# A scheduler's rule for where float32 subtractions run: beside GpSimd's instructions, and on GpSimd

## The chip, the core and the metric

The kernel runs on one core of a Trainium2 chip. The metric is the device time of one execution in microseconds. The core's engines are TensorE (PE; its weight loads are shown as PEld), VectorE (DVE), ScalarE (ACT), GpSimd (POOL) and SyncE (SP, which here issues nearly all DMAs).

## What is computed

Decay attention over 4 batches, 8 heads, 576 positions and a head width of 64, and then two feed-forward layers, all in float32. Cut to what matters:

```python
scores = scale * q @ k.T                       # per batch and head
scores = where(causal, -1e9, scores + cum[:, None] - cum[None, :])
attn = softmax(scores);  x = attn @ v          # 2304 tokens x 512
h1 = x @ w1_in;   y1 = (h1 * sigmoid(1.702 * h1)) @ w1_out       # 512 -> 2048 -> 512
h2 = y1 @ w2_in;  out = (max(h2, 0) + alpha * min(h2, 0)) @ w2_out
```

## The kernel before, in words

A matmul operand is split into two float32r tiles: a rounded copy (the high part) and the difference of the source and that copy (the low part). A product is three matmuls: high by high, high by low, low by high. So each operand costs a copy and a **float32 subtraction** of equal size, and where the Strassen form of a product is used (the last third of the first layer, and the second layer) there are more additions and subtractions to make its operands.

The program is written as a list of operations with read and write sets. `Plan.plan` orders it: at each step it takes, of the operations whose inputs are ready, the one that can start first. An operation has one or more alternatives, tuples of engine, estimated duration, a bias that is added to the end time when engines are compared, and a flag `port`. Operations with the flag share one resource, `free["port"]`: no two of them are planned at the same time, on whatever engine. VectorE's reads of PSUM are planned without it. The engines then execute their queues in the order that the plan gave; the times of the plan are not kept, only its order.

The places that the prediction speaks of:

- `a_sub` (the subtraction's alternatives): GpSimd with the flag; VectorE with a bias of `BS` = 200 ns and the flag. Once the attention phase and the last third of the first product are written down, the list `late` is filled, and from there on `a_sub` gives VectorE alone, with the flag.
- `exact` (lines 685 to 688) rebuilds a weight tile `wc` from its raw bits `wraw`: two ScalarE passes, a shift on VectorE (line 687) and an integer add on VectorE or GpSimd (line 688). `halves` then makes the weight's high and low part (`w`; the copy by line 513 or 515, the subtraction by line 518). 16 weight tiles are made so during the first 110 us, while attention runs.
- `split` makes `KA` and `QA`, the operands of the scores, out of the transposed `tk`; `gemm1` makes `xh` and `xl` out of the attention output `xr`, and multiplies them with `w` (line 1008). These matmuls are planned as background work that fills TensorE's gaps in the attention phase.
- `tail` is the Strassen form for the last 768 tokens of the first product. It starts when attention has ended: `st` (line 1115) are combinations of `xr`, `xt` the split operands; for each pair of weight tiles `tw` and `td` (line 1140) are sums of weights, `tb` the split form of `td`. Its products are line 1031, its PSUM sums line 1057. The rest of the background matmuls of line 1008 is interleaved with it.
- The matmuls of attention are lines 872 and 878 (scores), 952 (transposes) and 966 (times v); line 891 adds the mask on VectorE, line 900 is the exponential on ScalarE, and line 919 (VectorE or GpSimd) or 917 (ScalarE) scales the result.
- Where the plan of the first 130 us leaves TensorE idle, `run` puts filler matmuls in (line 484).

Of the kernel before, what the change touches and what calls it, by code (L numbers as in the profile page):

```python
# [12 lines left out]
ALU = mybir.AluOpType  # L13
# [3 lines left out]
BC = 0  # L17
WC = 0.6
WO_ = 0.0
BS = 200  # L20
WS = 0
BD = 300
WLAG = 2500.0
# [226 lines left out]
def kernel(  # L250
# [51 lines left out]
    plan = Plan()  # L302
    E = {"PE": nc.tensor, "DVE": nc.vector, "ACT": nc.scalar, "POOL": nc.gpsimd, "SP": nc.sync, "ACTQ": nc.scalar}
# [195 lines left out]
    def c_dve(n, fast=False):  # L499
        return n / (1.92 if fast else 0.96) + 68.0  # L500
# [4 lines left out]
    def c_act(n, ps=False):  # L505
        return n / 1.2 + (51.0 if ps else 93.0)

    def c_pool(n):
        return 2.1 * n + 200.0
# [19 lines left out]
    late = []  # L529

    def a_sub(n):
        if late:
            return [("DVE", c_dve(n), 0.0, True)]
        return [("POOL", c_pool(n), 0.0, True), ("DVE", c_dve(n), BS + WS * n, True)]

    plan.add(DMA(BH * S * 4), lambda e: nc.sync.dma_start(f_sb(), f.rearrange("b h s -> (b h) s")), (), [b_f], -100)

# [84 lines left out]
    for part, (lo, hi) in enumerate(((0, SPLIT), (SPLIT, S))):  # L622
        ts_ = [t for t in range(NKT) if lo <= t * P < hi]
        pri = -80 if part == 0 else A0 + P1PRI
# [45 lines left out]
    def hold(o, gate):  # L670

        if gate is not None and gate not in o.deps:
            o.deps.add(gate)
            gate.succ.append(o)

    def exact(src, pri, lpri=None, lag=0.0, gate=None):

        raw, w = Buf(p_raw8), Buf(p_wc)
        n = KT * P
        o = plan.add(DMA(P * n * 8), lambda e: nc.sync.dma_start(raw.ap.rearrange("p c n t -> p c (n t)"), src), (), [raw], pri if lpri is None else lpri, lag)  # L680
        hold(o, gate)
        low, high = lambda: raw.ap[:, :, :, 0], lambda: raw.ap[:, :, :, 1]
        wi = lambda: w.ap.bitcast(I32)

        plan.add([("ACT", c_act(n))], lambda e: nc.scalar.activation(w.ap, high().bitcast(F32), AF.Prelu, scale=2.0 ** -112, alpha=2.0 ** 32), [raw], [w], pri)
        plan.add([("ACT", c_act(n))], lambda e: nc.scalar.mul(low(), low().bitcast(U32), 2.0 ** -29), (), [(raw, 0)], pri)
        plan.add([("DVE", c_dve(n, True), 0.0, True)], lambda e: nc.vector.tensor_scalar(wi(), wi(), 3, None, op0=ALU.logical_shift_left), (), [w], pri)  # L687
        plan.add(a_sub(n), lambda e: E[e].tensor_tensor(wi(), wi(), low(), op=ALU.add), [raw], [w], pri)  # L688
        return w

    def halves(n, src, sb_, hi, lo, buf, key, pri, over=()):

        plan.add(a_copy(n), lambda e: copy(e, hi(), src()), sb_, [(buf, (key, 0)), *over], pri)
        plan.add(a_sub(n), lambda e: sub(e, lo(), src(), hi().bitcast(F32)), [*sb_, (buf, (key, 0))], [(buf, (key, 1)), *over], pri)

    def in_rows(w, m):
        return w[:, m * P:(m + 1) * P].bitcast(I32).rearrange("(c p) n -> p c n", p=P)

    def out_rows(w, m):
        return w[m * P:(m + 1) * P, :].bitcast(I32).rearrange("p (c n) -> p c n", c=KT)  # L700
# [21 lines left out]
    def split(T, w, big, keys, pri):  # L722
        hi, lo = Buf(None, big, 0), Buf(None, big, 1)
        plan.add(a_copy(w), lambda e: copy(e, hi.ap[:, :w], T.ap[:, :w]), [T], [(hi, x) for x in keys], pri)
        plan.add(a_sub(w), lambda e: sub(e, lo.ap[:, :w], T.ap[:, :w], hi.ap[:, :w].bitcast(F32)), [T, *((hi, x) for x in keys)], [(lo, x) for x in keys], pri)
        return hi, lo
# [461 lines left out]
    def first_weights():  # L1188
        over = {3: p_k0.bufs[:2], 4: p_k0.bufs[2:], 5: p_d0.bufs, 6: p_q0.bufs[:2], 7: p_q0.bufs[2:], 8: p_v0.bufs, 9: p_v0.bufs, **{m: p_r0.bufs[:4] if m < 13 else p_r0.bufs[4:] for m in range(10, NM)}}
        for m in range(NM):  # L1190
            WI[m] = Buf(wA)
            pri = A0 + WPRI + m * WSTEP
            w = exact(in_rows(w1_in, m), pri, A0 + WPRI - 1 + m * WSTEP, WLAG + (1000.0 if m < 4 else 0.0))
            halves(KT * P, lambda w=w: flat(w.ap), [w], lambda m=m: flat(WI[m].ap[:, 0]), lambda m=m: flat(WI[m].ap[:, 1]), WI[m], 0, pri, over.get(m, ()))
# [38 lines left out]
    for k in range(NM):  # L1233
        WO[k] = wb = Buf(wo[k >= WO0])
        pri = 1500.0 + k
        w = exact(out_rows(w1_out, k), pri)
        halves(KT * P, lambda w=w: flat(w.ap), [w], lambda wb=wb: wb.ap[:, 0], lambda wb=wb: wb.ap[:, 1], wb, 0, pri, [WI[k]])
# [64 lines left out]
    for p in range(NPAIR):  # L1302
        TS[p] = sw = Buf(wS)
        pri = 5000.0 + p
        w = [exact(in_rows(w2_in, m), pri, None, WLAG, Y[34 + 4 * p] if p < 6 else None) for m in (p, p + NPAIR)]
# [96 lines left out]
    for i, (t0, n) in enumerate(out_turn):  # L1402
# [4 lines left out]
        for k in range(NPAIR):  # L1407
            pri = base + k - 60
            raw, s_, hi, lo = Buf(p_R), Buf(p_S), Buf(p_hi[turn % 2]), Buf(p_lo[turn % 2])
# [96 lines left out]
```

## Time and profile before

| | before |
|---|---|
| median of 3 runs | 953.25 us (951.26 to 953.94) |
| the profiled execution, its own time | 951.31 us |
| its span | 949.6 us |
| TensorE clock granted | 0.998 of full speed |
| busy: PE, DVE, ACT, POOL | 939.9, 739.8, 561.2, 31.2 us |
| POOL instructions with a record | 46 |
| HBM read and written | 107.71 and 63.85 MB |

Matmuls are pipelined and the ends of their records are modelled, so a busy share of 99% of TensorE says that no long gap is shown, not that the engine is at its peak. How dense it is worked is seen from the number of matmuls in a stretch. On VectorE and ScalarE records of neighbours overlap by some 0.08 us, so what one instruction costs in a row of them is the distance between starts. An instruction that is held back by another engine's use of memory shows as a longer record, not as idle time.

### The profile page before, as it was taken

How to read it: one execution, taken by the hardware profiler on the slowest of the kernel's cores; microseconds unless marked ns; L12 is line 12 of the kernel's file. 1: busy time of each engine (PE TensorE's matmuls, PEld its weight loads, DVE VectorE, ACT ScalarE, POOL GpSimd, SP SyncE). 2: the span in 40 equal slices, each digit the busy share in tenths (PEclk: the TensorE clock that was granted, in tenths of full speed). 3: DMA queues.
4: the chain of work that ended last, by engine and by line, in shares of the span. 5: the costliest groups of instructions: out<-in, count | busy, mean ns of one | idle time of the engine just before them, and what ended most of it. 6: DMA issues, size and time to landing. Idle time of an engine off the chain costs nothing.

```text
span 949.6 us, 18126 instructions
## 1 busy us (share of the span) xinstructions
PE 939.9 (99%) x6517; PEld 873.0 (92%) x6517; DVE 739.8 (78%) x1771; ACT 561.2 (59%) x1238; POOL 31.2 (3%) x46
## 2 busy tenths in 40 slices
PE   8999999999999999999999999999999999999998
PEld 6789898889899999988888988999999999999998
DVE  5999997877759658755768876979569878898987
ACT  6999976777664538556776774556466623221212
POOL 1000010201001000000000000000000000000000
PEclk9999999999999999999999999999999999999999
DMA  7777764343211546558896784787638594443423
GB/s 151 172 185 190 180 158 97 85 92 73 59 52 65 183 159 226 157 174 327 299 323 198 257 257 151 257 307 288 244 124 319 187 398 164 139 150 96 155 79 100
DMA packets 179035, 172.78 MB, mean 182 GB/s; under 512 B 98320, under 2 KB 153760, under 8 KB 176640
## 3 DMA queue, kind: packets, MB, share of 16 engines
q1 hardware_dynamic: 178928, 171.61, 57.9%
q8 instruction: 51, 0.84, 0.4%
q14 instruction: 40, 0.33, 0.1%
q10 hardware_dynamic: 16, 0.01, 0.0%
HBM read 107.71 MB, written 63.85 MB: 181 GB/s over the span
## 4 chain that ended last, share of the span: by engine, by line
PE 89%; DVE 5%; DMA 1%; issue 0%; ACT 0%; DVEq 0%; SPq 0%; ACTq 0%
PE bk L1031 25%; PE bk L1252 21%; PE bk L1434 19%; PE bk L1008 12%; PE bk L966 4%; PE bk L952 4%; PE bk L878 3%; PE bk L872 1%; DVE w L518 1%; DVE wc L688 1%; DMA raw<-in_k_dram 1%; DVE eT L515 0%; DVE wc L687 0%; DVE tk L719 0%; DVE eb L891 0%
## 5 line engine op out<-in xcount | busy, mean ns | idle before, releaser
L1031 PE MATMUL bk<-x,wS 128*128 128x384 f32 x912 | 160.4, 334 | 0.0
L1031 PEld LDWEIGHTS bk<-x,wS 128*128 128x128 f32 x912 | 158.2, 188 | 0.7 <-DVE lx L1057 0.5
L1008 PE MATMUL bk<-xh,w 128*128 128x320 f32 (+2 forms) x640 | 150.2, 310 | 0.1
L1252 PE MATMUL bk<-lh,w 128*128 128x512 f32 (+1 forms) x640 | 146.9, 368 | 0.0
L1252 PEld LDWEIGHTS bk<-lh,w 128*128 128x128 f32 x640 | 112.7, 189 | 19.8
L1008 PEld LDWEIGHTS bk<-xh,w 128*128 128x128 f32 x640 | 108.9, 189 | 4.5 <-issue 1.7
L1008 PE MATMUL bk<-xl,w 128*128 128x320 f32 (+2 forms) x320 | 97.0, 303 | 0.4 <-DVE xl L518 0.4
L518 DVE TENSOR_TENSOR ll<-lx,lh 128x512 fp32r<-128x512 f32 (+1 forms) x80 | 50.9, 636 | 40.0 <-PE bk L1252 26.1
L1252 PE MATMUL bk<-ll,w 128*128 128x512 f32 (+1 forms) x320 | 81.2, 368 | 0.0
L513 ACT CAST x<-x 128x768 fp32r<-128x768 f32 (+3 forms) x41 | 33.4, 825 | 67.5 <-PE bk L1434 54.9
L1434 PE MATMUL bk<-wS,x 128*128 128x256 f32 x567 | 70.5, 283 | 0.0
L1218 ACT ACTIVATE lx<-lx 128x512 f32<-128x512 f32 (+1 forms) x80 | 46.9, 588 | 39.5 <-DVE ll L518 34.6
L1434 PEld LDWEIGHTS bk<-wS,x 128*128 128x128 f32 x567 | 69.1, 192 | 0.0
L1434 PE MATMUL bk<-wS,lh 128*128 128x256 f32 x378 | 68.7, 283 | 0.0
L1252 PEld LDWEIGHTS bk<-ll,w 128*128 128x128 f32 x320 | 57.0, 189 | 9.6
L1008 PEld LDWEIGHTS bk<-xl,w 128*128 128x128 f32 x320 | 60.5, 189 | 0.7 <-DVE xl L518 0.7
L513 ACT CAST lh<-x 128x768 fp32r<-128x768 f32 (+3 forms) x29 | 23.2, 805 | 62.9 <-PE bk L1434 48.3
L518 DVE TENSOR_TENSOR x<-x,x 128x768 fp32r<-128x768 f32 (+3 forms) x59 | 55.9, 979 | 4.1 <-ACT x L513 3.1
L1434 PEld LDWEIGHTS bk<-wS,lh 128*128 128x128 f32 x378 | 59.0, 192 | 0.0
L513 ACT COPY lx<-bk 128x384 f32<-128x384 f32 x72 | 34.3, 481 | 38.6 <-PE bk L1031 25.6
L1434 PE MATMUL bk<-wS,ll 128*128 128x256 f32 x189 | 53.5, 283 | 0.0
L513 ACT CAST lh<-lx 128x512 fp32r<-128x512 f32 (+1 forms) x68 | 38.9, 572 | 16.8 <-PE bk L1252 16.3
(204 smaller groups left out, 1976.4 us busy)
## 6 DMA issues: line engine op xcount, KB each, us to landing
h2scr<-lx SPq DMA_DIRECT2D x96, 192.0 KB, 3.9
wraw<-in_moe_w_in_dram SPq DMA_DIRECT2D x32, 512.0 KB, 5.6
wraw<-in_moe_w_out_dram SPq DMA_DIRECT2D x32, 512.0 KB, 6.3
lx<-h1scr SPq DMA_DIRECT2D x64, 256.0 KB, 4.2
x<-h2scr SPq DMA_DIRECT2D x32, 512.0 KB, 3.8
w2scr<-wS SPq DMA_DIRECT2D x5, 1792.0 KB
tscr<-wS SPq DMA_DIRECT2D x4, 1792.0 KB, 5.8
wS<-tscr SPq DMA_DIRECT2D x4, 1792.0 KB, 10.4
```

The costliest lines, as they stand in the source:

```text
L513: nc.scalar.copy(dst, src)
L518: E[e].tensor_tensor(dst, a, b, op=ALU.subtract)
L688: plan.add(a_sub(n), lambda e: E[e].tensor_tensor(wi(), wi(), low(), op=ALU.add), [raw], [w], pri)
L872: nc.tensor.matmul(o, x, y, start=i == 0, stop=i == 3)
L878: nc.tensor.matmul(pms[hh].ap[:, f0:f0 + c1 - c0], l, y.ap[r, c0:c1], start=i == 0, stop=i == 3, skip_group_check=True)
L952: nc.tensor.transpose(pt.ap[:, i * P:(i + 1) * P], view[j, hh](t * P, t * P + P), ident)
L966: nc.tensor.matmul(pb.ap[64 * hh:64 * hh + 64, x0:x1], vr.ap[:, t, hh], et.ap[:, c0:c0 + x1 - x0], start=t == 0 and hh not in seen, stop=t ...
L1008: nc.tensor.matmul(ph.ap[:, :n], w.ap[:, a, c, :], x[c // 2].ap[:, c % 2, :n], start=(c == 0 and j == 0), stop=(c == KT - 1 and j == 2))
L1031: nc.tensor.matmul(out.ap[:, :XH], wt(a, c), x.ap[:, b, c, :], start=(st and c == 0 and i == 0), stop=(c == 1 and i == 2), skip_group_chec ...
L1218: plan.add([("ACT", c_act(n))], lambda e: nc.scalar.activation(g.ap[:, :n], raw.ap[:, :n], AF.Gelu_apprx_sigmoid), [raw], [g], pri)
L1252: nc.tensor.matmul(py[d].ap[:, :n], w[:, a, d * P:(d + 1) * P], (lo if x else h).ap[:, :n], start=(k == 0 and (a, x) == (0, 0)), stop=(k = ...
L1434: nc.tensor.matmul(py[j].ap[:, t * HF:(t + 1) * HF], x.ap[:, q:q + P], w[:, o, a, :], start=(k == 0 and t == 0 and c == 0), stop=(k == NPA ...
```

## The change

```diff
-BS = 200
+BS = 1000
@@ a_sub
         if late:
             return [("DVE", c_dve(n), 0.0, True)]
-        return [("POOL", c_pool(n), 0.0, True), ("DVE", c_dve(n), BS + WS * n, True)]
+        return [("POOL", c_pool(n), 0.0, True), ("DVE", c_dve(n), BS + WS * n)]
@@ exact
-        plan.add(a_sub(n), lambda e: E[e].tensor_tensor(wi(), wi(), low(), op=ALU.add), [raw], [w], pri)
+        plan.add(a_sub(n) if late else [("POOL", c_pool(n), 0.0, True), ("DVE", c_dve(n), BS + WS * n, True)], lambda e: E[e].tensor_tensor(wi(), wi(), low(), op=ALU.add), [raw], [w], pri)
```

VectorE's alternative of a subtraction loses the flag (the plan may put it beside an instruction of GpSimd), and it is taken only where GpSimd would end more than 1000 ns later than it, instead of 200 ns. The integer add of `exact` keeps the flag and gets the new bias. No operation is added to or taken from the computation; the plan comes out in another order, and operations change engine. Of GpSimd's rows 48 become 126; VectorE's go from 1677 to 1594.

GpSimd while the weights are made, beside attention (`wc` and `wraw` are the weight rebuilt and its raw bits, `w` its low part, `xl` the low part of the attention output, `ea` the softmax weights, `Z` a helper of the scores). Its rows from the first one behind the set-up on, before:

```order
L688 TENSOR_TENSOR wc_499<-wc_499,wraw_368 128x512
L781 TENSOR_TENSOR Z_421<-QA_381,bm 128x256
L518 TENSOR_TENSOR w_99<-wc_732,w_99 128x512
L518 TENSOR_TENSOR w_1214<-wc_615,w_1214 128x512
L919 TENSOR_SCALAR ea_290<-ea_290,ms_360 128x128
L919 TENSOR_SCALAR ea_264<-ea_264,ms_265 128x128 x2
```

and now:

```order
L518 TENSOR_TENSOR xl_447<-xr,xh_437 128x2x256
L518 TENSOR_TENSOR xl_602<-xr,xh_596 128x2x256
L688 TENSOR_TENSOR wc_509<-wc_509,wraw_368 128x512
L688 TENSOR_TENSOR wc_576<-wc_576,wraw_378 128x512
L518 TENSOR_TENSOR w_660<-wc_509,w_660 128x512
L518 TENSOR_TENSOR w_660<-wc_576,w_660 128x512
L688 TENSOR_TENSOR wc_616<-wc_616,wraw_402 128x512
L518 TENSOR_TENSOR w_660<-wc_616,w_660 128x512
L518 TENSOR_TENSOR KA_243<-tk_682,KA_243 128x576
L688 TENSOR_TENSOR wc_509<-wc_509,wraw_368 128x512
```

Adds and subtractions of the weights, and those of `xl` and `KA`, have come over from VectorE; the small scalings of `ea` have gone to other engines.

GpSimd at the start of `tail` (the end of attention; behind the last scaling of `ea` before, behind the last `xl` of 640 columns now). Before:

```order
L1140 TENSOR_TENSOR td_3719<-tw_3695,w_578 128x256
L1140 TENSOR_TENSOR td_3719<-td_3719,w_578 128x256
L1140 TENSOR_TENSOR td_3719<-tw_3695,w_99 128x256
L1140 TENSOR_TENSOR td_3719<-tw_3695,td_3719 128x256
L1140 TENSOR_TENSOR td_3719<-td_3719,w_165 128x256
L1140 TENSOR_TENSOR td_3719<-td_3719,w_1214 128x256
```

and now:

```order
L1140 TENSOR_TENSOR tw_3677<-w_660 128x512
L518 TENSOR_TENSOR xt_3675<-xr,xt_3675 128x768
L1140 TENSOR_TENSOR td_3688<-td_3688,w_660 128x256
L1140 TENSOR_TENSOR td_3688<-tw_3677,td_3688 128x256
L518 TENSOR_TENSOR xt_3717<-xr,xt_3717 128x768
L1140 TENSOR_TENSOR td_3688<-td_3688,w_660 128x256
L1140 TENSOR_TENSOR tw_3677<-w_99 128x512
L518 TENSOR_TENSOR xt_3769<-st_3696,xt_3769 128x768
L518 TENSOR_TENSOR xt_3778<-xr,xt_3778 128x768
L1140 TENSOR_TENSOR td_3688<-w_660,td_3688 128x256
L1140 TENSOR_TENSOR td_3688<-td_3688,w_660 128x256
L518 TENSOR_TENSOR xl_447<-xr,xh_926 128x768
```

Four of the seven `xt`, one of the two `xl` and more of the weight sums are GpSimd's now, at the very start of the stage.

VectorE at the same place, from its last copy of `xr` on. Before:

```order
L518 TENSOR_TENSOR xt_3693<-xr,xt_3693 128x768
L1115 TENSOR_TENSOR st_3711<-xr 128x768
L1140 TENSOR_TENSOR td_3719<-tw_3695,w_578 128x256
L1115 TENSOR_TENSOR st_3722<-st_3711,xr 128x768
L1140 TENSOR_TENSOR td_3719<-td_3719,w_578 128x256
L1140 TENSOR_TENSOR td_3719<-tw_3695 128x256
L1140 TENSOR_TENSOR td_3719<-tw_3695,td_3719 128x256
L515 CAST xt_3746<-st_3711 128x768
L518 TENSOR_TENSOR xt_3733<-st_3722,xt_3733 128x768
L1140 TENSOR_TENSOR td_3719<-w_578,td_3719 128x256
```

and now:

```order
L1115 TENSOR_TENSOR st_3679<-xr 128x768
L1140 TENSOR_TENSOR td_3688<-tw_3677,w_660 128x256
L1115 TENSOR_TENSOR st_3696<-st_3679,xr 128x768
L1140 TENSOR_TENSOR td_3688<-tw_3677 128x256
L515 COPY gg_818<-bk_93 128x320
L518 TENSOR_TENSOR xt_3707<-st_3696,xt_3707 128x768
L1140 TENSOR_TENSOR td_3688<-w_660,td_3688 128x256
L1115 TENSOR_TENSOR st_3696<-xr,st_3696 128x768
L518 TENSOR_TENSOR xt_3728<-st_3679,xt_3728 128x768
L1115 TENSOR_TENSOR st_3679<-xr 128x768
L515 CAST xt_3769<-st_3696 128x768
L518 TENSOR_TENSOR tb_3758<-td_3688,tb_3758 128x1024
```

The chain of `td` that ends in the first `tb` now goes to and fro between the two engines: its second, fourth and seventh row here, and between them GpSimd's third, fourth and sixth row above.

## Rows read from the trace of the kernel before

**Rows 1.** The page's busy times of the whole span.

```profile
PE 939.9 (99%) x6517; PEld 873.0 (92%) x6517; DVE 739.8 (78%) x1771; ACT 561.2 (59%) x1238; POOL 31.2 (3%) x46
```

**Rows 2.** The chain that ended last, in order of time: start, us, what.

```profile
77.14 1.20 DVE w L518 x2
...
111.27 1.00 PE bk L1008 x5
...
285.30 5.47 PE bk L1008 x36
```

**Rows 3.** Three stretches: busy us and instructions of each engine, clock, DMA.

```profile
50.00:125.00 75.00, 74.50 (x652) 66.65 (x653) 74.75 (x239) 71.13 (x187) 5.80 (x6) 1.00 0.75 185
125.00:275.00 150.00, 148.98 (x1339) 132.83 (x1336) 112.26 (x424) 106.58 (x317) 13.27 (x13) 1.00 0.37 88
285.00:301.00 16.00, 16.00 (x111) 15.93 (x108) 15.60 (x23) 7.71 (x13) 2.19 (x2) 1.00 0.22 75
```

**Rows 4.** The filler matmuls of line 484 in the first of these stretches (PE, PEld).

```profile
50.00:125.00 75.00, 2.43 (x18) 2.17 (x18) 1.00 0.75 185
```

**Rows 5.** GpSimd's groups by form: busy us, mean ns of one, idle before.

```profile
L518 POOL TENSOR_TENSOR KA<-tk,KA 128x576 fp32r<-128x576 f32 x2 | 2.9, 1444 | 30.4 <-DVE ms L909 20.5 <-DVE KA L515 10.0
L518 POOL TENSOR_TENSOR w<-wc,w 128x512 fp32r<-128x512 f32 x2 | 2.6, 1296 | 46.4 <-DVE ms L911 24.8 <-ACT w L513 21.6
L1140 POOL TENSOR_TENSOR td<-w,td 128x256 f32<-128x256 f32 x1 | 0.7, 742 | 18.0 <-ACT wraw L686 18.0
```

**Rows 6.** VectorE's groups by form between 20 and 400 us.

```profile
L688 DVE CUSTOM_DVE_ANT_0 wc<-wraw,wc 128x1024 uint16<-128x1024 uint16 x31 | 20.9, 683 | 1.5 <-ACT wraw L686 1.2
L518 DVE TENSOR_TENSOR w<-wc,w 128x512 fp32r<-128x512 f32 x28 | 19.1, 687 | 0.7 <-ACT w L513 0.4
L518 DVE TENSOR_TENSOR tb<-td,tb 128x1024 fp32r<-128x1024 f32 x8 | 9.7, 1218 | 1.1 <-ACT tb L513 1.0
L1140 DVE TENSOR_TENSOR td<-td,w 128x256 f32<-128x256 f32 x13 | 5.4, 415 | 0.0
L518 DVE TENSOR_TENSOR xt<-xr,xt 128x768 fp32r<-128x768 f32 x3 | 2.8, 948 | 0.0
```

**Rows 7.** In order of time, POOL and DVE at 64 us: start, us, what.

```profile
64.14 1.30 POOL L518 TENSOR_TENSOR w<-wc,w 128x512 fp32r<-128x512 f32 x1 [24.79 <-DVE ms L911]
64.05 0.76 DVE L719 STREAM_TRANSPOSE tk<-raw 128x576 f32<-128x576 f32 x1
```

**Rows 8.** The same at 184 us.

```profile
184.52 2.00 POOL L518 TENSOR_TENSOR QA<-tk,QA 128x576 fp32r<-128x576 f32 x1 [5.18 <-ACT QA L513]
184.57 0.67 DVE L518 TENSOR_TENSOR xl<-xr,xh 128x512 fp32r<-128x512 f32 x1
185.17 1.50 DVE L919 TENSOR_SCALAR ea<-ea,ms 128x256 f32<-128x256 f32 x1
183.90 0.34 DVE L919 TENSOR_SCALAR ea<-ea,ms 128x256 f32<-128x256 f32 x1
```

**Rows 9.** The same at 375 us.

```profile
375.55 0.74 POOL L1140 TENSOR_TENSOR td<-w,td 128x256 f32<-128x256 f32 x1 [18.05 <-ACT wraw L686]
375.79 1.05 DVE L1140 TENSOR_TENSOR tw<-w 128x512 f32<-128x512 f32 x1
```

**Rows 10.** The start of `tail`, VectorE in order of time.

```profile
294.43 1.22 DVE L518 TENSOR_TENSOR tb<-td,tb 128x1024 fp32r<-128x1024 f32 x1
296.44 0.68 DVE L1140 TENSOR_TENSOR tw<-w 128x512 f32<-128x512 f32 x1
297.04 0.55 DVE L515 CAST xt<-st 128x768 fp32r<-128x768 f32 x1
```

**Rows 11.** TensorE there, in order of time.

```profile
297.80 1.23 PE L1031 MATMUL bk<-xt,w 128*128 128x384 f32 x6
298.87 0.31 PE L1008 MATMUL bk<-xh,w 128*128 128x320 f32 x1
299.74 2.27 PE L1031 MATMUL bk<-xt,tb 128*128 128x384 f32 x12
```

## The prediction

> **What bounds the kernel now.** I began with the busy times of the whole span [rows 1]: TensorE's records cover 99% of it, VectorE 78%, ScalarE 59%, GpSimd 3%. So the end is TensorE's work plus whatever holes hide in its modelled records. The chain of waits in order of time [rows 2] says where holes can be: until 111 us it runs mostly through VectorE (its pieces are the subtractions and adds for the weights), from 111 us on through TensorE, in unbroken pieces. In the stretch from 50 to 125 us VectorE is busy 74.75 of 75 us and ScalarE 71.13; from 125 to 275 us 112 and 107 of 150 [rows 3].
>
> How much TensorE loses in the first of them: it does 652 matmuls in 75 us, 18 of them fillers that compute nothing [rows 3, 4], so 634 / 75 = 8.45 a us; from 125 us on, with a like mix and TensorE as the bound, 1339 / 150 = 8.93. It works 5.3% below its rate there, which is 4.0 us. That is all that a free VectorE could give back in this stretch; before 50 us the change moves little.
>
> **What moves.** By the order, 15 integer adds and 10 low parts of weights (512 columns), 14 of `KA` and `QA` (576), 7 `xl`, 4 `xt` (768), 17 `td`, 3 `tw` and 4 `Z` go from VectorE to GpSimd; 7 scalings leave GpSimd, and ten large scalings go from VectorE to ScalarE. In a row of its own kind an instruction costs VectorE its mean less the 0.08 us of overlap [rows 6]: 0.60 for 512 columns, 0.34 for 256, 0.87 for 768, and 0.67 for 576 (between them). VectorE is relieved of 25 x 0.60 + 14 x 0.67 + 4.7 (`xl`) + 4 x 0.87 + 17 x 0.34 + 3 x 0.60 + 4 x 0.34 = 42 us. GpSimd takes 1.30 us for 512 columns, 1.44 for 576, 0.74 for 256 [rows 5]; 768 is not there and lies on their line at 1.86. It gains 25 x 1.30 + 14 x 1.44 + 10.2 + 4 x 1.86 + 17 x 0.74 + 3 x 1.30 + 2.4 - 4.5 = 85 us, from 31 to about 116.
>
> **Do the two engines run beside each other?** The plan now supposes so for subtractions. At 184.52 us GpSimd's subtraction of 576 columns takes 2.00 us instead of 1.44, while VectorE's of 512 columns runs its usual 0.67; then VectorE's scaling, 0.34 us when alone, takes 1.50 and ends 0.15 us after GpSimd [rows 8]. At 375.79 us a `tw` on VectorE takes 1.05 instead of 0.68, behind a GpSimd instruction that is running [rows 9, 10]. So two inputs in SBUF on VectorE, or its fast scaling, and a GpSimd subtraction exclude each other, and whoever comes second waits. Only instructions such as the 32-wise transpose run at full speed beside it: 0.76 and 1.30 us [rows 7]. From rows 9 the wait ends about 0.13 us before GpSimd's record does (1.05 - 0.68 = 0.37 us after 375.79, against 376.29). The Trainium skill ("SBUF — State Buffer", section "Who interferes with whom") states the same exclusion for a VectorE instruction with two SBUF inputs against a GpSimd instruction that reads SBUF, and has the loser blocked for the whole of the other's instruction. By that rule each handover below costs 0.13 us more, and the sum comes out 1 us longer; I go by the row.
>
> **The sum, stage by stage.**
>
> Weights and attention, 36 to 125 us: 18 us of VectorE's relief falls here, but ScalarE, 71.13 of 75 us busy [rows 3], gets some of the scalings, and about 40 us of GpSimd's new work holds the shared access. VectorE's shifts, copies, scalings and some ten subtractions that the plan now lays beside GpSimd must wait for it, up to 1.2 us each. Below, the stage gives back the 4.0 us; above, ten collisions of 0.6 us, all on the path, cost 6. I take 0: relief and blocking about cancel, and ScalarE caps what is left.
>
> Attention, 125 to 285 us: VectorE is idle a quarter of the time and GpSimd gets some 25 subtractions. 0, at most +2 if a softmax step waits for one and TensorE has no background matmul at hand.
>
> The start of `tail`: here the count is plain, since nearly every VectorE instruction has two SBUF inputs. T0 is TensorE's first matmul behind the last of attention, 285.30 us before [rows 2]. Before, 84 background matmuls and two products come ahead of the first product with `tb`, which starts at 299.74, 14.4 after T0 [rows 11]; six matmuls of a product take 1.07 us (297.80 to 298.87), so one background matmul takes 0.147. `tb` was ready at 294.43 + 1.22 = 295.65, 4.1 us early [rows 10]. VectorE was busy 15.60 of these 16 us [rows 3]: the 4.1 us were the margin.
>
> Now 90 background matmuls and one product come ahead: TensorE wants `tb` at 90 x 0.147 + 1.07 = 14.3 us after T0. Ahead of the end of `tb` stand on VectorE four `st` and two `xt` of 0.87, three `td` of 0.34, a cast of 0.47 [rows 10] and `tb` itself, 1.14: 7.85 us. On GpSimd there stand two `tw` (2 x 1.30), two `xt` (2 x 1.86) and three `td` (3 x 0.74): 8.5. They cannot overlap but for the 0.13 us at seven handovers: 7.85 + 8.5 - 0.9 = 15.5, about 15.6 with the first wait. So `tb` is 1.3 us late. A PSUM sum of line 1057, queued on VectorE behind a blocked `td`, costs 0.4 more. Then the `xl` that is now GpSimd's: behind `tb` come two `xt` of 1.86 and one of 0.87, four `td` on VectorE (1.36) and two on GpSimd (1.48), a `tw` (0.60) and `xl` itself (1.86), 9.9 - 0.4 = 9.5; it ends at 25.1 and is wanted, by the same count of matmuls, at 22.3 + 1.7 of earlier delay: 1.1 late. The second `xl` comes behind `tb` of the next pair (1.14), two `td` on VectorE and three on GpSimd (0.68 + 2.22) and a `tw` (0.60), with its own 0.87 at 30.2, wanted at 26.5 + 2.9: 0.8 late. Together **3.6 us** on the path. Below it is 0, if GpSimd's first `tw` and `xt` run ahead of T0 and the margin stays. Above it is 7, if at four places the waiting instruction is let in only after a second one of the other engine (0.87 each). I take the count, which rests on rows 8 and 9 as they are.
>
> The rest of `tail`, 325 to 385 us: `td` on GpSimd costs 0.74 for 0.34, but TensorE is fed there with slack. 0, at most +2. From 400 us on the order is the same but for neighbours that change places: 0.
>
> Sum: +3.6 us. The profiled execution took 951.31 us, of a span of 949.6, and would take 954.9; against the median of the runs, 953.25, which is 1.9 above the profiled one, it is **956.9 us** (953.25 + 3.6).
>
> **Rivals.**
>
> *VectorE's relief decides (faster).* The 4.0 us come back, and `tail` keeps its margin because GpSimd's first `tw` and `xt` start while the last matmuls of attention still run. For it: VectorE is the chain until 111 us, and 18 us of it go. Against: rows 8 and 9, and ScalarE, which is as full. The Trainium skill ("Perfetto Trace Analysis", section "Optimizing Scalar/DVE Operations") says for this that moving work to GpSimd may make sense when VectorE is saturated, and against it that the two share a port; the trace bears out the second. It decides if the tail's stall is under 1 us: 953.25 - 4.0 = 949.3 us, 0.2.
>
> *Both cancel (no change).* TensorE's queue absorbs the waits: 1 to 2 us back in the weight stage, 2 to 3 lost in `tail`. 953 to 955 us, 0.3.
>
> *The shared access becomes the bound of the weight stage (much slower).* 40 us of GpSimd and VectorE's own SBUF instructions, at 0.6 us for each collision, push the weights behind the background matmuls: +6 there, +2 in attention, +3.6 in `tail`: 965 us, 0.12.
>
> *The change does not do what it says*, that is, subtractions do not run beside GpSimd's instructions: that is part of my forecast, and no case of its own.
>
> **How the numbers follow.** The forecast (+2.9 to +8 us) has 0.38. About 0.3%, 2.9 us, is what a measurement of this kernel can tell from no change. Slower by more: 0.38 + 0.12 = 0.5; within: 0.3; faster by more: 0.2. The range goes from the full relief, 949.3, to the last rival, 965.
>
> **What would show it.** Right: GpSimd's busy time near 116 us; VectorE's scalings and subtractions with records of over 1 us beside GpSimd's; GpSimd's 768-column instructions at 1.9 us or more; the chain at the end of attention going through POOL and DVE, with TensorE waiting for `tb` or `xl` for some us around 290 to 315 us. Wrong: no wait of TensorE there, or more than 8.7 matmuls a us between 50 and 125 us with the fillers taken off, which is the first rival; a chain that runs through POOL `w` and `wc` before 120 us, which is the third.

## The result and the profile after

The change takes **963.15 us** (median of 5 runs, 962.7 to 965.64) against 951.6 for the kernel before in the same measurement: a ratio of 1.0118, 95% interval 1.0106 to 1.0131. It is slower, and inside the range, but by 11.6 us and not by 3.6: the forecast had the direction and a third of the size. The direction was in part luck: all of the 3.6 us were put at the start of `tail`, and most of the 11.6 are lost ahead of it. The profiled execution has a span of 961.2 us, again 11.6 more, so the trace shows all of it.

The page of the change, busy times and then the chain that ended last, by engine:

```profile
PE 941.5 (98%) x6507; PEld 871.8 (91%) x6507; DVE 734.3 (76%) x1686; ACT 566.0 (59%) x1247; POOL 132.6 (14%) x122
...
PE 84%; DVE 12%; issue 1%; DMA 1%; SPq 1%; POOL 1%; ACT 0%; DVEq 0%; ACTq 0%; POOLq 0%
```

GpSimd works 132.6 us where 31.2 stood [rows 1]; I had said 116. Its own instructions grew, too: 14 `td` of 256 columns take 0.96 us in the mean, where [rows 5] has 0.74. VectorE has 85 instructions fewer and is only 5.5 us less busy: the first sign that those it kept became longer. The same stretches as [rows 3], in the change:

```profile
50.00:125.00 75.00, 69.19 (x620) 60.49 (x619) 73.42 (x218) 69.35 (x184) 41.47 (x32) 1.00 0.74 179
125.00:275.00 150.00, 146.94 (x1285) 130.42 (x1283) 105.33 (x390) 109.16 (x316) 31.13 (x26) 1.00 0.37 88
285.00:301.00 16.00, 16.00 (x127) 15.57 (x126) 10.33 (x14) 7.22 (x14) 7.70 (x6) 1.00 0.22 74
```

From 50 to 125 us TensorE is idle for 5.8 us of 75 (0.5 before), and VectorE is still busy 73.42 us with 218 instructions where it did 239 in 74.75. Before, 2.43 us of TensorE's work there were fillers [rows 4], and the change has none, so its useful matmuls cover 2.9 us less. What TensorE waited for, between 25 and 290 us:

```profile
PE bk L952 <- DVE ec L919: 2.0, 2, 1.8
PE bk L966 <- ACT eT L513: 1.9, 2, 1.3
PE bk L952 <- DVE ed L919: 1.9, 3, 0.8
PE bk L878 <- DVE ms L891: 1.5, 1, 1.5
```

(The columns are us in total, times, longest.) These are attention's own steps, as are the four shorter waits behind them, and no weight is among them.

Three landmarks place the 11.6 us. T0, the first matmul behind the last of attention, comes at 292.04 us instead of 285.30 [rows 2], and 12 background matmuls fewer are done by then (660 against 672): 6.74 + 12 x 0.147 = **8.5 us lost before T0**. The first matmul of line 1252 starts at 379.4 instead of 369.2: another **1.7 us at the start of `tail`**. The first of line 1434 starts at 775.6 instead of 764.0: another **1.4 us in the second layer**. From there on nothing is lost.

How one collision looks, GpSimd and VectorE in order of time (start, us, what):

```profile
121.86 1.43 POOL L518 TENSOR_TENSOR KA<-tk,KA 128x576 fp32r<-128x576 f32 x1 [3.29 <-PE bk L1008]
...
122.04 1.93 DVE L518 TENSOR_TENSOR xl<-xr,xh 128x640 fp32r<-128x640 f32 x1
...
123.59 1.78 POOL L518 TENSOR_TENSOR xl<-xr,xh 128x640 fp32r<-128x640 f32 x1 [0.31 <-ACT xh L513]
...
124.23 1.24 DVE L909 TENSOR_SCALAR ms<-ms 128x2 f32<-128x2 f32 x2
```

VectorE's `xl` starts 0.18 us behind GpSimd's `KA`, seems to get access when that ends (123.29; `xl` ends 0.68 us later), and takes 1.93 us. Then two instructions of line 909, **two elements wide** on each partition, stand for 1.24 us beside GpSimd's next one; what they compute is what the softmax's scalings want next.

### The profile page after: what moved, and what is told of

The parts are those of the page before. It is cut to its first block, busy times and chain, and to the rows that moved or that the text cites. A ratio compares the mean times of both kernels' runs of the same rounds, so it can differ in the third digit from the quotient of the medians.

```text
span 961.2 us, 18125 instructions
## 1 busy us (share of the span) xinstructions
PE 941.5 (98%) x6507; PEld 871.8 (91%) x6507; DVE 734.3 (76%) x1686; ACT 566.0 (59%) x1247; POOL 132.6 (14%) x122
## 4 chain that ended last, share of the span: by engine, by line
PE 84%; DVE 12%; issue 1%; DMA 1%; SPq 1%; POOL 1%; ACT 0%; DVEq 0%; ACTq 0%; POOLq 0%
PE bk L1031 23%; PE bk L1252 21%; PE bk L1434 19%; PE bk L1008 10%; PE bk L966 4%; PE bk L952 3%; PE bk L878 3%; PE bk L872 1%; DVE ms L909 1%; DVE tk L719 1%; DVE ea L891 1%; DVE eb L891 1%; DVE td L1140 1%; DVE KA L518 1%; DVE ed L919 1%
## 5 line engine op out<-in xcount | busy, mean ns | idle before, releaser
L1008 PE MATMUL bk<-xh,w 128*128 128x320 f32 (+2 forms) x640 | 148.0, 309 | 0.1
L513 ACT COPY lx<-bk 128x384 f32<-128x384 f32 x72 | 34.2, 479 | 38.5 <-PE bk L1031 25.1
```

The costliest lines, as they stand in the source:

```text
L513: nc.scalar.copy(dst, src)
L1008: nc.tensor.matmul(ph.ap[:, :n], w.ap[:, a, c, :], x[c // 2].ap[:, c % 2, :n], start=(c == 0 and j == 0), stop=(c == KT - 1 and j == 2))
```

## The experiments

Four causes were to be told apart. **S** (shared access): a GpSimd instruction that reads SBUF holds up VectorE's in-order queue. **L** (late results): a subtraction ends later on GpSimd, and its reader waits. **P** (plan): the new rule changes the order of everything, and that order is worse. **A** (flag): it is the missing flag, not the larger share of GpSimd.

For S there is a measure. In the run e12 below GpSimd does nothing during attention, so each form of VectorE instruction has its undisturbed mean there. *Held up* is VectorE's busy time in the first 310 us less what its instructions would take at those means. It is good to some 2 us: e17, with GpSimd as empty as in e12, should have 0 and has 1.9. *GpSimd* is the number of its instructions behind the set-up at the start, in the whole run.

| run | plan of | GpSimd | held up, us | time, us | ratio to before (95%) |
|---|---|---|---|---|---|
| before | before | 28 | 4.0 | 951.6 to 954.1 | 1 |
| the change | the change | 104 | 29.6 | 963.15 | 1.0118 (1.0106 to 1.0131) |
| e1 bias only | own | 143 | 17.4 | 959.59 | 1.0064 (1.0040 to 1.0087) |
| e2 flag only | own | 51 | 14.8 | 963.18 | 1.0102 (1.0073 to 1.0132) |
| e3 plan of the change, subtractions on VectorE | the change | 10 | not worked out | 965.33 | 1.0137 (1.0112 to 1.0161) |
| e4 never GpSimd, planned anew | own | 16 | not worked out | 956.49 | 1.0044 (1.0029 to 1.0060) |
| e5 old plan, new GpSimd set | before | 107 | 34.6 | 964.94 | 1.0122 (1.0097 to 1.0148) |
| e5a the same, attention only | before | 75 | 29.6 | 962.93 | 1.0113 (1.0087 to 1.0138) |
| e5d old plan, subtractions on VectorE | before | 13 | not worked out | 954.81 | 1.0014 (0.9998 to 1.0031) |
| e6 bias 150 | own | 26 | not worked out | 954.75 | 1.0010 (0.9996 to 1.0025) |
| e8 shadow subtractions, first form | before | 148 | not worked out | 971.09 | 1.0190 (1.0164 to 1.0215) |
| e9 shadow fills, first form | before | 268 | not worked out | 964.79 | 1.0127 (1.0095 to 1.0159) |
| e12 GpSimd empty | before | 0 | 0 | 955.07 | 1.0025 (1.0014 to 1.0037) |
| e13 shadow subtractions | before | 141 | 17.2 | 971.72 | 1.0196 (1.0178 to 1.0215) |
| e14 shadow fills | before | 282 | 4.5 | 958.46 | 1.0060 (1.0041 to 1.0079) |
| e15 scratch of 257 columns | before | 0 | not worked out | 957.87 | 1.0055 (1.0034 to 1.0076) |
| e10 before, no line 909 | before | 28 | 3.0 | 950.86 | 0.9981 (0.9968 to 0.9994) |
| e11 the change, no line 909 | the change | 104 | 25.1 | 959.48 | 1.0066 (1.0044 to 1.0089) |
| e16 no line 909, planned anew | own | 39 | 4.8 | 956.0 | 1.0030 (1.0016 to 1.0045) |
| e17 the same, no GpSimd | own | 0 | 1.9 | 952.7 | 0.9999 (0.9988 to 1.0009) |

### The two halves of the change

```diff
 e1:  BS = 1000, and in a_sub the flag stays:
+        return [("POOL", c_pool(n), 0.0, True), ("DVE", c_dve(n), BS + WS * n, True)]
 e2:  the change with
+BS = 200
```

> Only the bias is raised to 1000; every subtraction keeps the exclusive flag, so the planner sets none of them beside a flagged VectorE instruction. It gives GpSimd 143 subtractions and 0 of these rules differ otherwise (the change: 104; before: 16). Theory (GpSimd's reading of SBUF holds up VectorE's in-order queue, so that the time follows the number of GpSimd subtractions): slower than the change, 963 to 970 us, since the real engines leave the planned times and the flag guards only planned ones. Rival A (the missing flag does the harm, the planner sets instructions side by side that exclude each other): at the time of the kernel before plus the tail's 1.7, 951 to 954. Rival B (the new order of the weights, first background matmul at 51 instead of 40 us): 960 to 964, like the change.

> Only the flag is taken from the subtractions; the bias stays 200. GpSimd gets 47 subtractions (the change 104, before 16). Theory (time follows the number of GpSimd subtractions): a third of the change's loss, 954 to 957 us. Rival A (the missing flag itself does the harm): 960 to 964, like the change. Rival B (order of the weights): somewhere between, no number.

(The counts in these two texts are of different things. Of subtractions and additions alone GpSimd has 15 before, 94 in the change, 134 in e1 and 36 in e2.) The time does not follow the number on GpSimd. e2, with half as many, is as slow as the change; e1, with the most, is faster than either, though slower than before. Held-up time for each GpSimd instruction of the same 310 us (25 before, 91 in e1, 38 in e2, 72 in the change) is 0.16 us before and 0.19 in e1, where the flag stands, and 0.39 in e2 and 0.41 in the change, where it is gone: the flag halves the harm, which is A in part. It does not make a large share free: e2 is in A's range, but e1 is in none of its three. The stretch from 40 to 150 us, of before, of the change and of e1:

```profile
40.00:150.00 110.00, 109.37 (x959) 97.02 (x957) 107.27 (x355) 99.40 (x272) 7.02 (x8) 1.00 0.72 175
```

```profile
40.00:150.00 110.00, 101.29 (x893) 87.53 (x892) 103.67 (x320) 97.61 (x262) 54.49 (x43) 1.00 0.69 167
```

```profile
40.00:150.00 110.00, 107.47 (x968) 93.36 (x966) 100.23 (x336) 105.17 (x281) 65.52 (x49) 1.00 0.68 161
```

GpSimd is busier in e1 (65.52 us) than in the change, and TensorE keeps 107.47 of 110 us where the change has 101.29. e1 loses elsewhere: its first background matmul comes at 54.3 us (before: 40.0; the change: 51.3), and 48 fewer of them are done when attention ends. By the landmarks e1 loses 6.0 us before T0 and 3.2 behind it. e2 loses 4.7 before T0 and 5.1 at the start of `tail`: it is as slow as the change, but not at the same place. In e2 TensorE's largest wait between 25 and 330 us is for `xl`, most of it at the start of `tail`:

```profile
PE bk L1008 <- DVE xl L518: 4.8, 2, 3.3
```

### Plan and engine crossed

e3 keeps the change's plan and issues its 94 subtractions on VectorE. e5 keeps the plan of before and issues the same 94 on GpSimd; e5a only the 54 of them that belong to weights and attention (7 of these were there before, so 47 move); e5d takes the 15 of before off GpSimd. e4 lets the old planner choose VectorE alone, and e6 changes its bias slightly.

```diff
 e3, in sub (and likewise in the additions of a_sub):
+        e = "DVE" if e == "POOL" else e
 e5, e5a, e5d, in Plan.run of before; GP and DV are lists of operations:
+            eng = "POOL" if o.seq in GP else "DVE" if o.seq in DV else eng
 e4, in a_sub of before:       e6, in before:
-        if late:              -BS = 200
+        if True:              +BS = 150
```

> The planner's result of the change is kept to the instruction: order on every engine, fillers, buffers; but the 104 subtractions and additions that it gave to GpSimd are issued on VectorE at the place where the plan starts them. Theory (GpSimd beside VectorE costs): the loss goes, 950 to 955 us, though VectorE has 104 instructions more (about 62 us of them at the 0.6 us that a 512-column subtraction takes on VectorE). Rival B (the new order, the later weights and the ten scalings more on ScalarE cost): stays at 960 to 965. Rival C (VectorE's relief was real and wanted, only something else ate it): worse than the change, 966 or more.

> The planner of the kernel before, but a subtraction has VectorE as its one choice (0 of them on GpSimd; before 16 until the end of the first layer). Theory: at the kernel before or a little faster, 948 to 952 us. Rival C (GpSimd's share relieves VectorE): slower than before by a good part of 16 x 0.6 us, 955 to 960.

> The crossed half of the run with the change's plan on VectorE: the plan of the kernel before is kept on every engine (order, fillers, buffers), but each of the 94 subtractions and additions that the change gives to GpSimd is issued there, at the place where the old plan starts it. Theory S (shared access: a GpSimd instruction that reads SBUF holds VectorE up, whatever the order): most of the change's loss comes back, 959 to 966 us. Theory P (the new plan's order is what costs, since the run with that order and no subtraction on GpSimd took 965.3): 949 to 955 us. Theory L (the longer chain: a result comes 0.7 us later from GpSimd than from VectorE, at 94 places that the old order did not leave room for): between, 955 to 960, with waits for the weights and for xl, KA, QA by name.

> As the run above, but of the 94 only the 54 of the weights and of attention (the weights' sum and low part, KA, QA, xl), not those of the block's operands and of the sums and differences of weights at the start of the tail. Theory S: 957 to 961, nearly all of the loss lies before 285 us. Theory P: 950 to 954.

> The plan of the kernel before, its 15 subtractions on GpSimd issued on VectorE instead. Theory S: 950 to 953, no loss since 15 x 0.6 us is little. Theory P: the same. If this is 956 or more, VectorE has no room for even 15 and the run with the change's plan on VectorE says nothing of the order.

> The kernel before with the bias 150 for 200, nothing else: GpSimd's share is nearly the same (18 instructions against 21 until attention's end, 5 against 6 after it), but the planner's choices elsewhere fall out differently by chance. Theory P in its strong form (the kernel before stands on a lucky order, any other costs): 955 to 962 us. Theory S: within 0.3% of the kernel before, 950 to 955.

e3 looked like the end of S: no subtraction on GpSimd, and 965.33 us, where S had 950 to 955. e5a turned that round: the plan of before, to the instruction, with 47 more subtractions on GpSimd, takes 962.93, even more than S had (957 to 961). It has the same order as before, so its landmarks compare directly: T0, the first of line 1252 and the first of line 1434 all come 11.2 us late, so all of it is lost before T0. Where GpSimd takes them, then, the old order loses as much as the new; the new order is not needed for the loss. But e3 says that the new order is no better without GpSimd: it was made for a VectorE that is relieved, and with the 94 back there it loses on VectorE's waiting line,

```profile
50.00:125.00 75.00, 67.88 (x582) 57.18 (x579) 74.88 (x242) 67.33 (x181) 2.14 (x3) 1.00 0.74 175
```

with VectorE at 74.88 of 75 us and TensorE at 67.88. The two losses do not add, so "plan" and "engine" are no shares of the 11.6 us. e6 speaks against a kernel before that stands on a lucky order, and e5d against a gain from its 15 subtractions on GpSimd: neither differs from it by more than the measurement tells. e4 missed the theory's 948 to 952 us and lies in the range of its rival, that GpSimd's small share relieves VectorE; e12 below, with the plan of before and nothing on GpSimd, is 2.7 us slower than before as well. So for the kernel before this rival stands.

The profiled execution of e4 is the slowest of its eight, 3.3 us over their median. In it T0 comes 7.9 us later than before with the same 672 background matmuls done. A large part is lost before 50 us: the granted clock is 0.81 from 25 to 50 us, a mix of TensorE's two levels (2.4 and 1.2 GHz), and TensorE is busy 20.77 of 25 us; it had stood idle for 2 of the 5 us from 30 on and again from 40 on, where the clock fell. GpSimd has little to do with it. First before, then e4:

```profile
25.00:50.00 25.00, 24.41 (x207) 18.53 (x205) 23.50 (x88) 23.79 (x73) 2.03 (x2) 1.00 0.74 160
```

```profile
25.00:50.00 25.00, 20.77 (x138) 15.70 (x137) 20.04 (x72) 18.51 (x52) 0.95 (x1) 0.81 0.71 152
```

What the two engines do to each other in e5a is seen on VectorE's groups of the first 310 us. First before, then e5a, of the instructions that did not move:

```profile
L909 DVE TENSOR_SCALAR ms<-ms 128x2 f32<-128x2 f32 x64 | 11.5, 182 | 1.0 <-ACT eb L900 0.9
...
L919 DVE TENSOR_SCALAR ec<-ec,ms 128x512 f32<-128x512 f32 x22 | 10.1, 478 | 0.0
...
L911 DVE RECIPROCAL ms<-ms 128x2 f32<-128x2 f32 x64 | 9.7, 155 | 0.2
```

```profile
L909 DVE TENSOR_SCALAR ms<-ms 128x2 f32<-128x2 f32 x64 | 21.8, 343 | 4.8 <-ACT eb L900 3.3 <-ACT ec L900 1.5
...
L919 DVE TENSOR_SCALAR ec<-ec,ms 128x512 f32<-128x512 f32 x22 | 13.2, 620 | 0.1
...
L911 DVE RECIPROCAL ms<-ms 128x2 f32<-128x2 f32 x64 | 9.8, 155 | 0.4
```

The two-element additions of line 909 nearly double, the scalings of line 919 grow by a third, the reciprocals not at all. VectorE waits as well, for ScalarE (line 900) and for GpSimd's `QA` (from 40 to 150 us), and TensorE for GpSimd's low parts of weights (from 25 to 300 us):

```profile
DVE ms L909 <- ACT eb L900: 2.4, 3, 1.9
...
DVE Z L781 <- POOL QA L518: 1.3, 1, 1.3
```

```profile
PE bk L1008 <- POOL w L518: 1.5, 3, 0.8
```

So L has a part here: 1.3 and 1.5 us by name. Whether S alone would do it needed a run in which nobody reads GpSimd's results.

### Shadows: GpSimd works, and nobody waits for it

Beside each of VectorE's subtractions of weights, `KA` and `QA`, GpSimd copies one column of an operand (which sets the moment) and then works on a scratch tile. e8 and e9 do so in the old plan as it is, at 40 places; e12 first takes everything else off GpSimd, and e13 and e14 add the shadows to it, at 47 places. The code is cut to what matters.

```diff
+    shade = lambda x: plan.shadow and [nc.gpsimd.tensor_copy(scr[:, 256:257], x[:, 0:1])] + WORK
 e8, e13:  WORK = [nc.gpsimd.tensor_tensor(scr[:, 0:256], mf, mf, op=ALU.subtract) for i in range(2)]
 e9, e14:  WORK = [nc.gpsimd.memset(scr[:, 0:256], float(i)) for i in range(5)]
 e12: no shadow; e12 to e14: scr of 320 columns; e8, e9, e15: of 257
```

> The plan of the kernel before; VectorE keeps every subtraction that it had there. Beside 40 of them (the weights' sums and low parts, KA, QA, where the change would have used GpSimd) GpSimd now also does two subtractions of 256 columns whose result nobody reads, after copying one column of the subtraction's operand, which sets the moment. Nothing in the program waits for GpSimd's extra work. Theory S (shared access): slower than the kernel before by as much as the 54 moved ones, or more, since VectorE is not relieved: 962 to 975 us, and VectorE's tiny scalings (line 909) are over 0.25 us in the mean instead of 0.18. Theory L (only the later results cost): 951 to 956.

> The same, but instead of the two subtractions GpSimd fills the same 256 columns five times with a constant: it writes SBUF and reads nothing. If only GpSimd's reading of two inputs shuts VectorE out: 951 to 956 us. If any GpSimd instruction does: as the run with subtractions, in proportion to GpSimd's busy time. Theory L: 951 to 956.

Both came out slow, and neither was clean. In the old plan GpSimd keeps the low parts of two weights, and these now stood behind the shadows in its queue; TensorE's wait for them, in e8 and in e9:

```profile
PE bk L1008 <- POOL w L518: 3.4, 1, 3.4
```

```profile
PE bk L1008 <- POOL w L518: 5.1, 2, 4.7
```

They do show what L can cost by itself: an instruction behind others in GpSimd's queue. (Line 909 has a mean of 228 ns in e8; S had expected over 250.) In both, line 1252 also took 223.6 us from first to last matmul instead of 219.3. Hence the next four.

> The base of the next two: the plan of the kernel before with all 28 of GpSimd's subtractions, scalings and products issued on VectorE, and an unused scratch tile of 320 columns. GpSimd does nothing after its fills at the start. 952 to 957 us by every theory (15 of the 28 moved cost 0.14%).

> e12 with, beside each of the 47 subtractions of the weights, KA and QA on VectorE, a copy of one column and two subtractions of 256 columns on GpSimd into the scratch tile, whose result nobody reads. Theory S (shared access): 6 to 15 us over e12, and VectorE's instructions of unchanged form longer by 15 to 25 us in sum. Theory L (late results): as e12, within 2 us, since nobody waits for GpSimd.

> e12 with five fills of 256 columns on GpSimd in place of the two subtractions, about as long in sum. If it is GpSimd's reading that shuts VectorE out: within 2 us of e12. If writing does as well: like e13. Theory L: as e12.

> e12 with the scratch tile of 257 columns (1028 bytes) in place of 320 (1280), which shifts the address of what lies behind it. If that is what made line 1252's matmuls 395 ns: 4 us more than e12, between 380 and 600 us. If the shadows did: as e12, and 389 ns.

e13 settles S against L. Nobody waits for GpSimd, VectorE does what it did in e12, and the span is 970.4 us against 953.2: **17.2 us** (16.7 between the medians, over the 6 to 15 expected), for 17.2 us of held-up VectorE. That both agree to the digit is luck: the profiled e13 has a lower mean clock than e12 (0.996 against 1.0), and the one of its four runs with 0.999 takes 970.42 us, 15.4 over e12's median. So it is 15 to 17 us for 17. Matmul by matmul (both runs have the same order), e13 is 12.6 us behind at e12's 125 us, for 11.6 held up by then, and 17.5 behind at the end of attention, for 16.9.

e14's fills, with GpSimd busy as long, hold VectorE up by 4.5 us and cost 4.5 (957.7 against 953.2; 3.4 between the medians), over the 2 us that were expected if only reading shuts VectorE out, and far less than e13. VectorE's groups in e12, then in e13 and e14:

```profile
L518 DVE TENSOR_TENSOR w<-wc,w 128x512 fp32r<-128x512 f32 x16 | 10.8, 678 | 0.0
...
L909 DVE TENSOR_SCALAR ms<-ms 128x2 f32<-128x2 f32 x64 | 9.9, 157 | 0.9 <-ACT eb L900 0.9
...
L687 DVE TENSOR_SCALAR wc<-wc 128x512 int32<-128x512 int32 x19 | 7.7, 411 | 0.0
```

```profile
L518 DVE TENSOR_TENSOR w<-wc,w 128x512 fp32r<-128x512 f32 x16 | 14.7, 923 | 0.0
...
L909 DVE TENSOR_SCALAR ms<-ms 128x2 f32<-128x2 f32 x64 | 12.7, 201 | 0.9 <-ACT eb L900 0.9
...
L687 DVE TENSOR_SCALAR wc<-wc 128x512 int32<-128x512 int32 x19 | 9.4, 502 | 0.0
```

```profile
L909 DVE TENSOR_SCALAR ms<-ms 128x2 f32<-128x2 f32 x64 | 10.9, 173 | 0.9 <-ACT eb L900 0.9
...
L518 DVE TENSOR_TENSOR w<-wc,w 128x512 fp32r<-128x512 f32 x16 | 10.7, 674 | 0.0
...
L687 DVE TENSOR_SCALAR wc<-wc 128x512 int32<-128x512 int32 x19 | 9.0, 483 | 0.0
```

Held-up time is lost at about full price, up to 125 us, where VectorE is full, and behind, where it is idle for a quarter of the time. GpSimd's subtractions hold up both kinds of instruction, its fills only those with one full input tile (line 919 by 2.1 us in sum, the shifts by 1.4, line 909 and the copies by 1.0 each): `w` on VectorE, with two inputs, keeps its 0.68 us beside them. The Trainium skill ("SBUF — State Buffer", section "Who interferes with whom") states this: VectorE with two SBUF inputs contends with a GpSimd instruction that reads SBUF and not with one that only writes, while VectorE's two-port modes, which `copy`, `cast` and `tensor_scalar` can enter, contend with GpSimd. The trace agrees for the first (678, 923 and 674 ns above) and fits the second (shifts: 411, 502 and 483). e15 explains the rest of e8 and e9: it has no shadow and shows the slower line 1252 (223.6 us again); its time is 2.8 us over e12's (1.4 between the spans), where I expected 4.

### Line 909, and room on VectorE

```diff
 e10 (before), e11 (the change):
-  lambda e, j=j: nc.vector.tensor_scalar_add(ms.ap[:, 6 + 2 * j:8 + 2 * j], ms.ap[:, 6 + 2 * j:8 + 2 * j], 1e-9)
+  lambda e: None
 e16 (before): the whole plan.add of line 909 is out
 e17: e16, with VectorE (and ScalarE, for line 919) as the choices of a_sub, a_scale and Z
```

> The kernel before without the 64 instructions of line 909 (the addition of 1e-9 to the sums of the softmax is left out; each sum holds exp(0) = 1, to which float32 adds 1e-9 without effect). They take 11.5 us of VectorE in the first 310 us. TensorE waits only some 2 us between 50 and 285 us, so the gain is bounded by that and by the first 50 us: 949 to 953 us.

> The change without the same 64 instructions (the addition of 1e-9 is left out, as above). Theory S: line 909 is the instruction that GpSimd holds up most (64 instructions, 21.8 instead of 11.5 us where only GpSimd's share was changed) and every softmax row waits for it, so a good part of the change's loss comes back: 956 to 960 us. Theory P (the order costs): no more than the kernel before gains from it, 960 to 963.

> The kernel before with line 909 taken out of the planner's list (the addition of 1e-9 to the softmax sums is left out), so that it plans anew; it gives GpSimd 18 or so subtractions more than before until the first layer. Leaving the instructions out of the old plan gave 0.19%. Theory S: the relief is worth about the same, but the added GpSimd subtractions take it back: 951 to 956 us. Theory P (a plan's order is mostly chance): anything from 948 to 958.

> As the run above, but no subtraction, scaling or product has GpSimd as a choice (0 of them there). Theory S: as fast as the run above or faster, 948 to 953 us. If GpSimd's relief of VectorE is worth something net: slower than it, 954 or more.

Taking line 909 out gives 0.4 to 0.5% in the change (ratios 1.0118 and 1.0066; 963.15 to 959.48 us) and 0.19% in the kernel before: by the spans 2.9 us against 1.3. It is dearer where it is held up, as S has it, though not far beyond the noise, and it is less than half of the loss. e16, at the upper end of what S expected, has a lesson: it has 11 instructions more on GpSimd (26 subtractions against 15, where the expectation had 18 more) and 64 fewer on VectorE, and is slower than before. With GpSimd forbidden (e17) the same planner is 3.3 us faster than e16 and level with before, as S expected. Of all that ran, e10 is the fastest: 950.86 us, faster than the kernel before by 0.06 to 0.32% and than the change by 1.3%. It leaves out adding 1e-9 to sums that are at least 1.

## Why the prediction was wrong in size

**Weights and attention: failed.** "I take 0 ... relief and blocking about cancel" for 36 to 125 us, and 0 for 125 to 285. It was 8.5 us together. The mechanism was read rightly off [rows 8, 9]; what was wrong is the sum that was made with it. I counted ten collisions of 0.6 us, as the upper bound, and named shifts, copies and scalings. In the change 20 VectorE instructions between 36 and 125 us are over 0.2 us longer than in e12, by 15.2 us in sum, and none was before. In the first 310 us the trace has 29.6 - 4.0 = 25.6 us more held-up time, some 20 of them ahead of T0. The 64 additions of line 909 alone hold 18.5 - 11.5 = 7 us of it, and I had not listed them, since they move two elements:

```profile
L909 DVE TENSOR_SCALAR ms<-ms 128x2 f32<-128x2 f32 x64 | 18.5, 294 | 3.5 <-ACT eb L900 2.0 <-ACT ec L900 1.2 <-ACT ea L900 0.3
```

For 125 to 285 us I had argued that VectorE is idle a quarter of the time; e13 loses 5 us there all the same. And "before 50 us the change moves little" was wrong: the first background matmul comes 11.4 us later.

Relief and blocking are not the same coin. In VectorE's own time they do nearly cancel: ahead of T0 its instructions would need 27.6 us less than before at their undisturbed means, against the 20 us held up. But the relief is not worth its time. What GpSimd took over are weights, `KA` and `QA`, which the plan could place freely; what was held up are mostly the steps of the softmax, for which ScalarE and TensorE wait in turn. In the change ScalarE's scalings (line 917) wait for line 911 for 7.7 us between 40 and 150 us, where they waited 1.1 before:

```profile
ACT ea L917 <- DVE ms L911: 4.7, 4, 2.3
ACT eb L917 <- DVE ms L911: 2.7, 3, 1.7
```

That held-up time costs about full price is shown (e13, e14); that the relief falls on work off the path is my reading of the waits, and was not run by itself. What the relief is worth can be estimated, if held-up time has that price everywhere. e5a relieves VectorE of 28.8 us ahead of T0, is held up 26.5 more than before and comes 11.3 late, so the relief brought some 15 of 28.8. e3 against the change, with the same plan, gives VectorE 33 us back, is held up 21 us less and comes 3.6 late at T0: there the relief was worth some 24 of 33. It counts, at half to three quarters of its time.

**Start of `tail`: right collisions, half the size, another wait.** 1.7 us for 3.6. In order of time, first from the chain, then instruction by instruction:

```profile
297.27 2.00 DVE td L1140
...
303.99 1.13 DVE tb L518
...
318.60 1.50 DVE xl L518
320.15 4.28 PE bk L1008 x23
```

```profile
306.30 1.23 PE L1031 MATMUL bk<-xt,tb 128*128 128x384 f32 x6
...
312.15 0.74 POOL L1140 TENSOR_TENSOR td<-td,w 128x256 f32<-128x256 f32 x1
...
312.93 1.05 ACT L513 CAST tb<-td 128x1024 fp32r<-128x1024 f32 x1 [5.95 <-POOL td L1140]
...
313.88 0.47 ACT L513 COPY u2t<-bk 128x384 f32<-128x384 f32 x1
...
314.40 1.34 PE L1031 MATMUL bk<-xt,tb 128*128 128x384 f32 x6 [1.08 <-ACT u2t L513]
```

`tb` is ready at 305.12, and 14.3 us after T0 is 306.3, when TensorE does take it: it was in time. My lower bound named the reason, GpSimd's first instructions ahead of T0. Its `tw` ran at 280.81 in 1.29 us and its first `xt` from 291.11 in 1.84. With these off, the 15.6 us of the count are 13.4, and 13.1 were measured: the collisions are as counted (a `td` of 2.00 us for 0.34). The wait came where the sum had no term. At 314.40 TensorE waits 1.08 us for ScalarE's copy `u2t` of a PSUM sum, which stands in ScalarE's queue behind the cast of the second `tb`, and that had waited for a `td` on GpSimd. The first `xl` cost nothing that shows, the second about 0.2 us (its matmul starts 0.41 us behind the one before, where 0.17 is usual). The rest of the 1.7 us is not placed.

**Rest of `tail` right, second layer wrong by 1.4.** From 379.4 to 598.7 us nothing is added. In the second layer TensorE waits 1.0 us for line 1057, where the order is the same but for neighbours. The run e5a, with the order of before, loses nothing there; e3, with the order of the change and no subtraction on GpSimd, loses the same 1.4 us. So it goes with the new order and not with GpSimd's share; which of the neighbours does it stays open.

**The rivals.** The first (VectorE's relief decides) and the second (both cancel) are out. The third had the right cause, shared access, and the right stages (6 + 2 us against 8.5), but the wrong path: it let the weights come late, while TensorE's waits name the softmax. That its sum of 11.6 us is the measured one is luck, since its 3.6 for `tail` stand for 1.7 there and 1.4 in the second layer. It had 0.12, and the two rows of collisions were grounds for more: in a stage where VectorE is busy 74.75 of 75 us there is no idle time for held-up instructions to fall into.

**The signs.** Records over 1 us on VectorE beside GpSimd's, and 768 columns at 1.9 us or more (three `xt` with a mean of 2.15), were there. A wait of TensorE for `tb` or `xl` of some us was not; it waited the 1.08 us for `u2t`. The first rival's sign was not there either: 620 matmuls in 75 us, none of them a filler, are 8.3 a us. A chain through GpSimd's `w` and `wc` before 120 us, which I had set as the third rival's sign, is there once:

```profile
82.75 1.84 POOL wc L688
```

It is the wrong sign for that rival's cause: held-up time shows in VectorE's records and in who waits for them.

## What to carry to other kernels

Before moving work from a full VectorE to GpSimd, list every VectorE instruction that shares access with it, the two-element ones too, and ask who waits for each: held-up time was paid about one for one here (15 to 17 us for 17), the relief by an estimate at half to three quarters of its time. Two sums in the engine's time that cancel are then a loss. A small share may still pay, as in the kernel before (e12 without it is 0.25% slower). If a planner is to use both, let it know the exclusion: with it GpSimd cost VectorE 0.16 to 0.19 us for each instruction, without it 0.39 to 0.41. A test for such a cause is a shadow: let the second engine do the work with no reader.

## What the runs showed of the hardware

- A two-element addition on VectorE is held up like a large one (two in 1.24 us; mean 157 ns with GpSimd empty). The reciprocal of the same tile is not (155 ns in before and in e5a).
- GpSimd's fills held VectorE up by 4.5 us in 78.5 us of their own time, its subtractions by 17.2 in 71.5 (the copies of one column that set the moment are in both runs, and not in these times).
- TensorE's rate changed with the size of a tile that nobody uses. With a scratch tile of 257 columns instead of 320, which shifts the addresses behind it, and nothing else, the matmuls between 425 and 525 us and between 800 and 900, e12 above and e15 below:

```profile
L1252 PE MATMUL bk<-lh,w 128*128 128x512 f32 x293 | 73.9, 389 | 0.0
...
L1434 PE MATMUL bk<-wS,x 128*128 128x256 f32 x294 | 36.4, 283 | 0.0
```

```profile
L1252 PE MATMUL bk<-lh,w 128*128 128x512 f32 x286 | 73.6, 395 | 0.0
...
L1434 PE MATMUL bk<-wS,x 128*128 128x256 f32 x300 | 36.3, 279 | 0.0
```

  Line 1252 lost 3.5 us from first to last matmul (220.1 to 223.6), line 1434 gained 2.3 (181.3 to 179.0). That it is the shift is not shown by itself, and which address does it was not tried.
